# AV on shared query rows and transposes in transpose mode by 64x128 tiles, four head pairs in one burst

## The chip, the cores and the metric

The kernel runs on one core of one Trainium2 chip. The metric is the device time in microseconds of one execution; the kernel before has a median of 320.39 us in three runs (319.56 to 322.47). Each kernel has one profiled execution besides, from which all views of the profile come.

The engines are called as the profile calls them: PE is TensorE's matrix multiplication, PEld its weight load, DVE is VectorE, ACT ScalarE, POOL GpSimd, SP the SyncE queue that issues transfers.

## The reference

An attention of two parts and, on its result, a dense network of two layers. All inputs and the output are fp32; there are 8 images of 576 tokens, 8 heads of 64.

```python
def _attn_ref(q, k, v):
    B, H, S, D = q.shape
    factor = 4
    Sd = S // factor
    scale = 1.0 / np.sqrt(D)
    ...
    q_d = q.reshape(B, H, Sd, factor, D).mean(axis=3)
    k_d = k.reshape(B, H, Sd, factor, D).mean(axis=3)
    v_d = v.reshape(B, H, Sd, factor, D).mean(axis=3)
    out_d = sm_attn(q_d, k_d, v_d)
    out_up = np.repeat(out_d, factor, axis=2)
    pos = np.arange(S)
    mask = np.abs(pos[:, None] - pos[None, :]) < factor
    scores = scale * np.matmul(q, k.transpose(0, 1, 3, 2))
    scores = np.where(mask, scores, -1000000000.0)
    ...
    out_local = np.matmul(attn, v)
    return (out_up + out_local).astype(np.float32)

def _moe_ref(x, w_in, w_out):
    h = x @ w_in
    g = h * (1.0 / (1.0 + np.exp(-1.702 * h)))
    return (g @ w_out).astype(np.float32)
```

The **down** part is full attention among 144 tokens, each the mean of four, and its result is repeated four times. The **local** part lets each token see the tokens up to 3 places off. x, 4608 tokens by 512 features, is their sum; the network goes 512 to 2048 to 512.

## The kernel before

**Dense layers.** The 4608 tokens are done in nine groups of 512 (`for g in range(n_groups)`). In a group `mm1` makes 16 blocks of 128 hidden features; a block is four 128x512 matmuls, one for each of the four `xT` tiles (features on partitions, tokens along the row), and an ACT `silu` takes it out of PSUM. The first two blocks of a group go together, xT by xT: eight matmuls, two on each xT in order of head pair. `mm2` then makes four blocks of 128 tokens, each of 16 matmuls, and ACT evacuates each block (`store`, L766) and SP sends it out. Blocks take turns on two PSUM banks, `PM`. In group 0 the order in mm2 is its own, with two of the blocks in `PA[0]`.

**Attention** of image g+1 is put between the dense matmuls of group g; image 0 has a version of its own ahead of group 0 (`av_local0`, `av_down0`, `transp_sum`, L518 to L606), which the change does not touch. `attention` gives a list of steps; `POS` (groups 1 to 6) and `POS_0` (group 0) say before which dense matmul each is emitted: a number under 16 is a block of mm1, a number n of 16 or more is matmul n - 16 of mm2. All engines run in the order in which the code emits their instructions; nothing is reordered by a scheduler. Semaphore waits are put in by the framework, which follows tiles: an instruction waits for whoever last used the tile that it touches.

Heads are done in four pairs (`hp`), heads 2hp and 2hp+1. The steps for one image are:

- `s_pe(0)`, `s_act(0)`, `s1`: scores of heads 0 to 3 and then 4 to 7 (L361, L375), local ones in five chunks of 2 x 60 query rows, down ones in three blocks of 48 keys; ACT takes the exponent (L415, L421), and DVE masks the local ones (L429).
- `avn`: AV for two pairs and its `normalise`. `av_local` (L440) multiplies chunk by chunk, `av_down` (L454) block by block, all in 64x64 tiles of the PE array, into a PSUM tile `o` of two banks: seven slots of 65 columns in each bank, the 65th being the sum of the weights. In the lower and the upper 64 partitions of a slot stand the two heads of the pair. `normalise` (L476) is a reciprocal and one multiplication on DVE, into `y` (bf16).
- `tr`: `transp` (L491) turns y by multiplication with an identity, 26 matmuls of 64x64 tiles for a pair, into an fp32 PSUM tile `x` of its own; the head goes to the right 64 partitions there. Then `copy_od` (L620) copies the down result, repeated four times, from `x` to `od` (fp32 in SBUF, two ACT copies), and `merge` (L637) adds the local result from `x` and `od` into `xT` (two DVE additions, of 570 and of 6 columns).

In groups 1 to 6 the last steps are `avn(0, 1)`, then AV of pairs 2 and 3 with the transposes of pair 0, then the transposes of pairs 1 to 3 with their additions. In group 0 they are `avn(0, 1)`, `tr(0)`, `tr(1)`, `avn(2, 3)`, `tr(2)`, `tr(3)`, each in a place of its own. Three PSUM tiles of two banks, `PA`, serve scores, `o` and `x` in turn (`ps_tile`); in group 0 `o` and `x` use two fixed ones of them. The second of the two first mm1 blocks uses a PA bank too.

DVE's other work for the next image (`prep_qk`, L267) is emitted at the head of the group; POOL pools q and k (L297, L301) and the values (L313, L316) and issues the loads of q and k. SP loads the values (L210, L233).

Of the kernel before, what the change touches and what calls it, by code (L numbers as in the profile page):

```python
# [19 lines left out]
def kernel(  # L20
# [410 lines left out]
    def av(b, hp, n=None):  # L431
        o = ps_tile(n)
        av_local(b, hp, o)
        av_down(b, hp, o)
        return o

    def banks(t):
        return t if t is PM else [t[:, u, :] for u in range(2)]

    def av_local(b, hp, o, chunks=range(5)):  # L440
        E, vb, o = es[hp], vbs[b % 2], banks(o)
        for i in chunks:
            for par in range(2):
                for j in range(2):
                    pos = j if par == 0 else 1 - j
                    nc.tensor.matmul(  # L446
                        o[par][64 * pos : 64 * pos + 64, 65 * i : 65 * i + 65],
                        lhsT=E[64 * par : 64 * par + 64, j, 60 * i : 60 * i + 64],
                        rhs=vb[64 * par : 64 * par + 64, i, 2 * hp + j, :],
                        start=True, stop=True,  # L450
                        tile_position=(64 * par, 64 * pos),
                    )

    def av_down(b, hp, o):  # L454
        Ed, vd, u, o = eds[hp // 2], vds[b % 2], hp % 2, banks(o)

        blocks = [(kc, x, 0) for kc in range(3) for x in range(2)]
        blocks += [(0, 0, 1), (0, 1, 1), (1, 0, 1), (2, 0, 1)]
        if True:
            for kc, x, c2 in blocks:  # L460
                for j in range(2):
                    pos = j if x == 0 else 1 - j
                    c0 = 65 * (5 + c2)
                    q0 = SD * kc + 48 * (min(x + c2, 1) + x)
                    last = x == c2 == 1
                    if last:
                        q0 = 0
                    nc.tensor.matmul(  # L468
                        o[j][64 * pos : 64 * pos + 64, c0 : c0 + 65],
                        lhsT=Ed[64 * j : 64 * j + 48, u, q0 : q0 + 64],  # L470
                        rhs=vd[64 * j : 64 * j + 48, kc, hp, :],
                        start=(kc == 0), stop=(kc == 2 or last),
                        tile_position=(64 * j, 64 * pos),
                    )

    def normalise(o):  # L476
        y = work.tile([128, 2, 7, D], BF16, name="y", tag="y", bufs=4)
        rc = work.tile([128, 2, 7, 1], FP32, name="rc", tag="rc")
        for xs in (slice(0, 1), slice(1, 2)) if o is PM else (slice(0, 2),):
            n = xs.stop - xs.start  # L480
            ov = (o[xs.start][:, None, :] if o is PM else o)[:, :, 0:455].rearrange(
                "p x (c e) -> p x c e", e=65
            )
            nc.vector.reciprocal(rc[:, xs], ov[:, :, :, 64:65])
            nc.vector.tensor_tensor(  # L485
                out=y[:, xs], in0=ov[:, :, :, 0:D],
                in1=rc[:, xs].to_broadcast([128, n, 7, D]), op=ALU.mult,
            )
        return y

    def transp(y, n=None):  # L491
        x = ps_tile(n)
        for i in range(5):
            for par in range(2):
                for j in range(2):
                    pos = j if par == 0 else 1 - j
                    c0 = 0 if (par == 1 or i == 0) else 3
                    c1 = 60 if (par == 0 or i == 4) else 57
                    nc.tensor.matmul(  # L499
                        x[64 * j : 64 * j + 64, par, 57 * i + c0 : 57 * i + c1],  # L500
                        lhsT=y[64 * pos : 64 * pos + 60, par, i, :],
                        rhs=ident(pos, 60, c0, c1),
                        start=True, stop=True,
                        tile_position=(64 * pos, 64 * j),
                    )
        for c2, xx in ((0, 0), (0, 1), (1, 0)):
            for j in range(2):
                pos = j if xx == 0 else 1 - j
                nc.tensor.matmul(  # L509
                    x[64 * j : 64 * j + 64, xx, 288 + 48 * c2 : 336 + 48 * c2],  # L510
                    lhsT=y[64 * pos : 64 * pos + 48, j, 5 + c2, :],
                    rhs=ident(pos, 48, 0, 48),
                    start=True, stop=True,
                    tile_position=(64 * pos, 64 * j),
                )
        return x
# [103 lines left out]
    def copy_od(x):  # L620
        od = work.tile([128, S], FP32, name="od", tag="od")
        for xx, t0, n in ((0, 0, 96), (1, 96, 48)):
            nc.scalar.copy(  # L623
                out=od[:, 4 * t0 : 4 * (t0 + n)].rearrange("p (t f) -> p t f", f=4),
                in_=x[:, xx, 288 : 288 + n, None].to_broadcast([128, n, 4]),
            )
        return od
# [351 lines left out]
```

## Time and profile before

| | |
|---|---|
| median of three runs | 320.39 us (319.56 to 322.47) |
| the profiled execution's own time | 320.13 us |
| its span, first to last instruction | 318.4 us |
| PE, PEld busy | 301.9 us (95%), 156.5 us (49%) |
| ACT, POOL, DVE busy | 184.9 us (58%), 138.7 us (44%), 130.3 us (41%) |
| mean granted TensorE clock | 0.995 |
| dense matmuls 128x512 (L717, L781) | 576 in each layer (the last block in halves) |
| transposes (L499, L509) | 560 and 168 matmuls |
| additions into xT (L644, L650) | 28 of 752 ns, 28 of 169 ns |

The profile gives for each instruction its start, its duration and what it waited for. The matmuls overlap in the array, so that a dense one lasts 379 ns in the profile while the next starts 216 ns after it; what an instruction costs the row is the distance between starts, not its duration. "Issue" is time in which an engine waited for nothing that the profile shows. The remainder of the execution's time, 1.7 us, lies before the first and after the last instruction.

### The profile page before, as it was taken

Reading aid. Unit: us, or ns where it says so; the run is one execution under the profiler, and the core shown is the slowest. Engines: PE = TensorE matmul, PEld = TensorE weight load, DVE = VectorE, ACT = ScalarE, POOL = GpSimd, SP = SyncE. Lnnn points to the kernel's source line nnn. Section 1 sums busy time; section 2 is a strip of 40 time slices with the busy share of each in tenths; the row PEclk is TensorE's granted clock in tenths of the full one; section 3 lists DMA queues with packets and bytes.
Section 4 is the critical chain, followed back from the end, with each engine's and each line's share of the span. In section 5 each row is a group of like instructions: output and inputs, shape, how many; then the busy total and the mean of one; then the engine's idle time right before and its main releaser. Section 6 shows DMA issues by size and latency. Waiting matters only on the chain.

```text
span 318.4 us, 10941 instructions
## 1 busy us (share of the span) xinstructions
PE 301.9 (95%) x4872; PEld 156.5 (49%) x4923; DVE 130.3 (41%) x219; ACT 184.9 (58%) x320; POOL 138.7 (44%) x170
## 2 busy tenths in 40 slices
PE   7699999999899999999999999999999999999995
PEld 4465454545454555445545454445445544444444
DVE  5855625831575047704780288017811650000000
ACT  5445782567546684659465846584667556415611
POOL 8773790099227940695059604980294000000000
PEclk9979999999999999999999999999999999999999
DMA  7999999999949923995299619961810210020011
GB/s 120 118 200 209 182 126 213 166 229 227 165 128 203 207 64 103 190 209 101 72 197 205 128 48 213 206 136 39 176 41 3 70 68 2 0 99 33 2 65 67
DMA packets 64078, 40.02 MB, mean 126 GB/s; under 512 B 44064, under 2 KB 55456, under 8 KB 64032
## 3 DMA queue, kind: packets, MB, share of 16 engines
q1 hardware_dynamic: 44496, 24.32, 37.3%
q0 software_dynamic: 19392, 14.95, 33.8%
q8 instruction: 38, 0.62, 0.9%
q14 instruction: 8, 0.07, 0.1%
q10 hardware_dynamic: 144, 0.07, 0.1%
HBM read 44.83 MB, written 9.44 MB: 170 GB/s over the span
## 4 chain that ended last, share of the span: by engine, by line
PE 91%; issue 3%; DMA 2%; DVE 1%; POOL 1%; ACT 1%; POOLq 0%
PE pm L781 35%; PE pm L717 35%; PE pa L717 4%; PE pa L365 2%; PE pa L377 2%; DMA qb<-in_q_dram 2%; PE pa L781 2%; PE pa L446 2%; PE pa L499 2%; PE pa L468 2%; PE pm L796 1%; PE pm L334 1%; PE pa L509 0%; PE pa L524 0%; DVE qT L267 0%
## 5 line engine op out<-in xcount | busy, mean ns | idle before, releaser
L717 PE MATMUL pm<-xT,w_in_bf 128*128 128x512 bf16 x495 | 118.2, 379 | 1.2 <-ACT xT L616 0.2
L781 PE MATMUL pm<-w_out_bf,gT 128*128 128x512 bf16 x499 | 114.4, 379 | 4.2 <-issue 4.1
L728 ACT ACTIVATE gT<-pm 128x512 bf16<-128x512 f32 x128 | 76.3, 598 | 43.7 <-PE pm L717 43.7
L717 PEld LDWEIGHTS <-w_in_bf 128*128 128x128 bf16 x576 | 55.7, 98 | 66.5 <-issue 0.5
L781 PEld LDWEIGHTS <-gT 128*128 128x128 bf16 x560 | 52.1, 98 | 60.1 <-issue 0.8
L429 DVE TENSOR_TENSOR es<-es,mask 128x600 bf16<-128x600 bf16 x28 | 17.6, 643 | 94.6 <-ACT es L415 93.8
L297 POOL TENSOR_TENSOR pq<-kT 128x576 f32<-128x576 bf16 x13 | 15.1, 1165 | 70.5 <-DVE kT L267 70.5
L766 ACT ACTIVATE osb<-pm 128x512 f32<-128x512 f32 (+2 forms) x35 | 20.5, 586 | 38.2 <-PE pm L781 30.3
L623 ACT COPY od<-pa 128x384 f32<-128x384 f32 (+1 forms) x56 | 19.0, 407 | 27.2 <-PE pa L509 20.7
L485 DVE TENSOR_TENSOR y<-pa,rc 128x896 bf16<-128x896 f32 x28 | 30.6, 1092 | 1.0
L415 ACT ACTIVATE es<-pa 128x600 bf16<-128x600 f32 x32 | 19.7, 668 | 9.5 <-PE pa L365 9.4
L644 DVE TENSOR_TENSOR xT<-pa,od 128x570 bf16<-128x570 f32 x28 | 21.0, 752 | 8.8 <-ACT od L623 8.8
L313 POOL TENSOR_TENSOR v<-v 112x512 f32<-112x512 f32 x18 | 23.0, 1279 | 0.0
L768 DVE TENSOR_SCALAR osb<-pm 128x128 f32<-128x128 f32 x1 | 0.3, 291 | 55.0 <-ACT osb L766 55.0
L267 DVE STREAM_TRANSPOSE kT<-kb 128x576 f32<-128x576 f32 x16 | 20.0, 1250 | 4.3 <-DMA kb<-in_k_dram 4.2
L267 DVE STREAM_TRANSPOSE qT<-qb 128x576 f32<-128x576 f32 x16 | 19.9, 1242 | 0.6 <-POOL kdT L301 0.2
L717 PE MATMUL pa<-xT,w_in_bf 128*128 128x512 bf16 x64 | 20.0, 379 | 0.0
L307 POOL CAST vb<-vf 128x2560 bf16<-128x2560 f32 x6 | 13.9, 2319 | 13.7 <-DMA vf<-in_v_dram 11.3
L365 PEld LDWEIGHTS <-kT 32*64 32x64 bf16 x1280 | 14.2, 104 | 7.7 <-issue 4.9
L365 PE MATMUL pa<-qT,kT 32*64 32x60 bf16 x1280 | 16.4, 198 | 1.3 <-DVE qT L267 1.3
L221 POOL DMA_DIRECT2D vb<-in_v_dram x20 | 13.7, 698 | 9.1 <-DMA w_in_bf<-in_moe_w_in_dram 4.0
L297 POOL TENSOR_TENSOR pq<-qT 128x576 f32<-128x576 bf16 x14 | 16.0, 1145 | 0.1
(90 smaller groups left out, 274.2 us busy)
## 6 DMA issues: line engine op xcount, KB each, us to landing
out_dram<-osb SPq DMA_DIRECT2D x35, 256.0 KB, 2.1
vf<-in_v_dram SPq DMA_DIRECT2D x60, 128.0 KB, 6.8
v<-in_v_dram SPq DMA_DIRECT2D x36, 192.0 KB, 5.5
kb<-in_k_dram POOLq DMA_DIRECT2D x16, 288.0 KB, 7.2
qb<-in_q_dram POOLq DMA_DIRECT2D x16, 288.0 KB, 8.6
w_in_bf<-in_moe_w_in_dram POOLq DMA_DIRECT2D x4, 512.0 KB, 7.2
w_out_bf<-in_moe_w_out_dram POOLq DMA_DIRECT2D x4, 512.0 KB, 12.9
vb<-in_v_dram POOLq DMA_DIRECT2D x20, 64.0 KB, 6.4
```

What stands on the lines that cost most here:

```text
L267: nc.vector.transpose(out=t32.rearrange("p (i c) -> p c i", c=18), in_=store[b, qd].bitcast(FP32).rearrange("p (c d) -> p c d", c=18),)
L297: nc.gpsimd.tensor_tensor(out=t1, in0=sv[:, :, 0:2, :], in1=sv[:, :, 2:4, :], op=ALU.add)
L313: eng.tensor_tensor(out=t1[0:112], in0=x[:, :, 0:2, :], in1=x[:, :, 2:4, :], op=ALU.add)
L365: nc.tensor.matmul(sp[r // 2][64 * par : 64 * par + 64, r % 2, 60 * i : 60 * i + 60], lhsT=kT[b, qd][rows, k0 : k0 + 64, a], rhs=qT[b, qd] ...
L415: nc.scalar.activation(out=es[2 * qd + u][:, :, 0:300], in_=sp[u][:, :, 0:300], func=AF.Exp, scale=inv_sqrt_d,)
L485: nc.vector.tensor_tensor(out=y[:, xs], in0=ov[:, :, :, 0:D], in1=rc[:, xs].to_broadcast([128, n, 7, D]), op=ALU.mult,)
L623: nc.scalar.copy(out=od[:, 4 * t0 : 4 * (t0 + n)].rearrange("p (t f) -> p t f", f=4), in_=x[:, xx, 288 : 288 + n, None].to_broadcast([128, ...
L644: eng.tensor_tensor(out=sub(xT[hp], t0 + 3, (57, 2), (114, 5), (1, 57)), in0=sub(x, 3, (509, 2), (57, 5), (1, 57)), in1=sub(od, 3, (57, 2) ...
L717: nc.tensor.matmul(acc, lhsT=w_in_bf[:, dmc, ffc * 128 : (ffc + 1) * 128], rhs=xT[dmc][:, g * TG : g * TG + TG], start=(dmc == 0), stop=(d ...
L728: nc.scalar.activation(out=gT[:, ffc, :], in_=acc, func=AF.Silu, scale=GELU_SCALE)
L766: eng.activation(out=osb, in_=ap, func=AF.Copy, scale=1.0 / GELU_SCALE)
L781: nc.tensor.matmul(ops[t], lhsT=gT[:, ffc, t * 128 : (t + 1) * 128], rhs=w_out_bf[:, ffc, :], start=(ffc == 0), stop=(ffc == n_ffc - 1),)
```

## The change

- **AV.** In `av` the two heads of a pair now share the partitions of a slot: the lower 64 partitions hold the even chunks and the upper ones the odd chunks, of both heads side by side. Chunk i of head j goes to slot `i // 2 * 2 + j` (one further on for the second half). The down blocks are laid out in the same manner, 64 query rows each, with the odd ends in slots of their own. The number and shape of the matmuls stay, their order is new.
- **normalise** writes the same columns, and an ACT copy of 64 columns on the upper partitions (`y[64:128, 5]` from `y[64:128, 12]`) is added behind it.
- **transp** takes 60 or 64 query rows of both heads in one instruction, 128 columns on a 64x128 tile, in transpose mode, into a PSUM tile seen as bf16. There are 13 for a pair, and two pairs share one PSUM tile (`x_pair`).
- **copy_od** and **merge**: od is bf16; the copies are of 64 and 80 columns repeated four times (96 and 48 before); the addition becomes three, of 456, 117 and 3 columns.
- **Steps.** All images have the same six steps: the transposes of all four pairs are one step at the end, and the additions follow. `POS` moves scores of heads 4 to 7 from 35 to 33, AV from 45 to 44 and the last step from 69 to 67; `POS_0` drops three steps, and has AV at 46 and 57 (46 and 56 before) and the transposes at 68.

```diff
     def av(b, hp, n=None):
         o = ps_tile(n)
-        av_local(b, hp, o)
-        av_down(b, hp, o)
+        E, Ed, vb, vd, u = es[hp], eds[hp // 2], vbs[b % 2], vds[b % 2], hp % 2
+
+        def local(i, par, j):
+            pos, c0 = i % 2, 65 * (i // 2 * 2 + j + par)
+            nc.tensor.matmul(
+                o[64 * pos : 64 * pos + 64, par, c0 : c0 + 65],
+                lhsT=E[64 * par : 64 * par + 64, j, 60 * i : 60 * i + 64],
+                rhs=vb[64 * par : 64 * par + 64, i, 2 * hp + j, :],
+                start=True, stop=True,
+                tile_position=(64 * par, 64 * pos),
+            )
+
+        def down(kc, j, pos, slot, q0, last=2):
+            nc.tensor.matmul(
+                o[64 * pos : 64 * pos + 64, j, 65 * slot : 65 * slot + 65],
+                lhsT=Ed[64 * j : 64 * j + 48, u, SD * kc + q0 : SD * kc + q0 + 64],
+                rhs=vd[64 * j : 64 * j + 48, kc, hp, :],
+                start=(kc == 0), stop=(kc == last),
+                tile_position=(64 * j, 64 * pos),
+            )
+
+        for i in (0, 2):
+            for j in range(2):
+                for par, e in ((0, 0), (1, 1), (1, 0), (0, 1)):
+                    local(i + e, par, j)
+        left = [(local, (4, par, j)) for j in range(2) for par in range(2)]
+        left += [(down, (kc, j, 0, 6 - 6 * j, 0)) for kc in range(3) for j in range(2)]
+        right = [(down, (0, j, 1, 5 + j, 64, 0)) for j in (1, 0)]
+        right += [(down, (kc, j, 1, 6 - 6 * j, 64)) for kc in range(3) for j in (1, 0)]
+        right += [(down, (kc, j, 1, 4 + j, 128)) for kc in range(3) for j in (1, 0)]
...
     def normalise(o):
...
+        nc.scalar.copy(out=y[64:128, 5, :], in_=y[64:128, 12, :])
+        return y
+
+    def x_pair(n=None):
+        t = ps_tile(n).rearrange("p x n -> p (x n)").bitcast(BF16)
+        t = t.rearrange("p (x n) -> p x n", x=2)
+        return [t[:, :, 512 * u : 512 * u + 512] for u in range(2)]
+
+    def transp(y, x):
+        def put(pos, c0, n, src):
+            nc.tensor.matmul(
+                x[:, pos, c0 : c0 + n], lhsT=src, rhs=ident(pos, src.shape[0], 0, n),
+                is_transpose=True, start=True, stop=True, tile_position=(64 * pos, 0),
+            )
+
+        for m in range(3):
             for par in range(2):
...
+                for pos in range(2 if m < 2 else 1):
+                    c0 = 8 * par + 2 * m
+                    put(pos, 120 * m + 60 * par, 60, y[64 * pos : 64 * pos + 60, c0 : c0 + 2, :])
+                if m == 2:
+                    c0 = 6 - 2 * par
+                    put(1, 240 + 64 * par, 64, y[64:128, c0 : c0 + 2, :])
+        put(0, 360, 64, y[0:64, 6:8, :])
...
     def copy_od(x):
-        od = work.tile([128, S], FP32, name="od", tag="od")
-        for xx, t0, n in ((0, 0, 96), (1, 96, 48)):
+        od = work.tile([128, S], BF16, name="od", tag="od")
+        for xx, c0, t0, n in ((0, 360, 0, 64), (1, 240, 64, 80)):
...
+    def merge(b, hp, x, od):
         t0 = b * S
...
+        row = x.ap[1][0]
+        for at, col, dims, from_x in (
+            (3, 3, ((228, 2), (114, 2), (1, 114)), ((120, 2), (row, 2), (1, 114))),
+            (459, 243, ((1, 117),), ((1, 117),)),
+            (0, 0, ((1, 3),), ((1, 3),)),
+        ):
+            nc.vector.tensor_tensor(
+                out=sub(xT[hp], t0 + at, *dims), in0=sub(x, col, *from_x),
+                in1=sub(od, at, *dims), op=ALU.add,
+            )
...
+        def tr():
+            for u in range(2):
+                st["x", 2 * u], st["x", 2 * u + 1] = x_pair(slots and slots[u])
+            for hp in range(HP):
+                transp(st["y", hp], st["x", hp])
+            for hp in range(HP):
+                merge(b, hp, st["x", hp], copy_od(st["x", hp]))
+
+        return [lambda: s_pe(0), lambda: s_act(0), s1, avn(0, 1), avn(2, 3), tr]
...
-    POS = [13, 16, 35, 45, 56, 69]
-    POS_0 = [16, 18, 30, 46, 52, 56, 65, 71, 75]
+    POS = [13, 16, 33, 44, 56, 67]
+    POS_0 = [16, 18, 30, 46, 57, 68]
     VDP_0 = 41
```

## The prediction

> **What bounds the kernel now.** I read the page first, then the chain that ended last in order of time, then timelines of single stretches, and last the rows of single lines.
>
> ```profile
> PE 301.9 (95%) x4872; PEld 156.5 (49%) x4923; DVE 130.3 (41%) x219; ACT 184.9 (58%) x320; POOL 138.7 (44%) x170
> ...
> PE 91%; issue 3%; DMA 2%; DVE 1%; POOL 1%; ACT 1%; POOLq 0%
> ```
>
> TensorE is the bound: busy for 95%, and 91% of the chain. The granted clock is 0.995. So an edit is worth what it takes out of, or puts into, the row of TensorE's instructions; DVE (41%) and ACT (58%) count only where TensorE waits for them. The chain in order of time, in one image (the columns: start, us, what):
>
> ```profile
> 148.25 2.10 PE pm L781 x9
> ...
> 151.34 2.32 PE pm L781 x10
> ...
> 154.85 2.75 PE pm L781 x12
> ...
> 158.54 2.32 PE pm L781 x10
> ```
>
> A 128x512 matmul of the dense layers takes one step of 0.2158 us (31 of them 6.69 us in the same view). Between them stand bursts of attention, and a burst costs the gap between the end of the last step and the next dense matmul: AV of two pairs 150.19 to 151.34, 1.15; AV of two pairs with one pair's transposes 153.50 to 154.85, 1.35; the transposes of three pairs 157.44 to 158.54, 1.10. Transposing an image thus costs 0.20 + 1.10 = 1.30 us. In group 0, which does image 1, each pair is transposed in a burst of its own:
>
> ```profile
> 50.56 1.03 PE L781 MATMUL pm<-w_out_bf,gT 128*128 128x512 bf16 x4
> ...
> 52.41 1.04 PE L781 MATMUL pm<-w_out_bf,gT 128*128 128x512 bf16 x4
> ...
> 53.94 1.67 PE L781 MATMUL pa<-w_out_bf,gT 128*128 128x512 bf16 x7 [0.16 <-issue]
> ...
> 56.81 1.24 PE L781 MATMUL pm<-w_out_bf,gT 128*128 128x512 bf16 x5 [0.16 <-issue]
> ...
> 58.75 0.81 PE L781 MATMUL pa<-w_out_bf,gT 128*128 128x512 bf16 x3
> ...
> 60.05 1.03 PE L781 MATMUL pa<-w_out_bf,gT 128*128 128x512 bf16 x4 [0.16 <-issue]
> ```
>
> By the same reckoning 0.99 (with a wait inside), 0.67, 0.63 (the next dense matmul is at 58.52) and 0.65: 2.94 us.
>
> **AV.** 40 matmuls for a pair before and 40 after, all of 64x65 or 48x65 on four 64x64 tiles, the busiest tile with 11 in both; only order and place change. Cost nothing. If the new order put neighbours on one tile, the last four would lose some 0.03 us each; I keep 0.2 us an image in the range.
>
> **The transposes.** 26 for a pair on four 64x64 tiles become 13 on two tiles of 64x128, seven on the first and six on the second. The 1.10 us of three pairs are 0.10 before the first, 0.65 in which 78 start (some 20 on each tile, so 0.033 us a step), and 0.35 from the last start to the next dense matmul. The trace has one row of 64x128 tiles:
>
> ```profile
> 21.86 0.27 PE L547 MATMUL pa<-vd,ed 48*128 48x65 bf16 x6
> ```
>
> Each takes 0.19, so six start within 0.08 us, three on each tile: 0.037 a step. With 60 columns for 65 I take 0.035. Four pairs are 28 steps on the fuller tile, 0.98 us, and the burst 0.10 + 0.98 + 0.35 = 1.43. Half the instructions, but half the tiles: the stream is no shorter. Transpose mode is not in this trace. Bounds: as dense as the 64x64 ones (52 x 0.0083 = 0.43, burst 0.88), or one after the other as the full-array transposes of L600 (eight in 0.29, 0.036 each; 1.87, burst 2.32).
> Group 0: 1.43 - 2.94 = **-1.51**. The six others: +0.13 each, **+0.8**.
>
> **What follows the burst.** The next layer's first eight matmuls go through the four xT in order, two on each, and nothing else is queued on TensorE behind them that could go first. For each pair ACT copies the down part to od, then DVE adds. The timeline of the burst above:
>
> ```profile
> 158.04 1.31 ACT L623 COPY od<-pa 128x384 f32<-128x384 f32 x4 [0.88 <-PE pa L509]
> 159.84 0.70 ACT L623 COPY od<-pa 128x384 f32<-128x384 f32 x2 [0.49 <-DVE xT L650]
> ...
> 158.77 0.75 DVE L644 TENSOR_TENSOR xT<-pa,od 128x570 bf16<-128x570 f32 x1 [1.02 <-ACT od L623]
> 159.56 0.17 DVE L650 TENSOR_TENSOR xT<-pa,od 128x6 bf16<-128x6 f32 x1
> ```
>
> Copies to the first add 0.73 (two copies, 576 elements before and after); adds 0.96 to their end; a copy that waited for an add starts 0.11 after it. Today DVE ends at 161.53, and the seventh matmul wants the last xT at 160.86 + 1.30 = 162.16: 0.6 us to spare.
>
> After the change two pairs share a PSUM tile, and in the built order pair 1's copy waits for pair 0's adds, pair 3's for pair 2's. The chain becomes copy, add, copy, add (with pair 2's copies beside pair 1's adds), copy, add. What an add costs is the open term. Three rows of tensor_tensor, beside L644 above:
>
> ```profile
> L429 DVE TENSOR_TENSOR es<-es,mask x28: 458/472/1884, 41.9 to 248.4; 128x600 bf16<-128x600 bf16 x28
> L485 DVE TENSOR_TENSOR y<-pa,rc x28: 1091/1092/1093, 50.2 to 254.8; 128x896 bf16<-128x896 f32 x28
> L129 DVE TENSOR_TENSOR dm<-dm 128x60 f32<-128x60 f32 x1 | 0.2, 220 | 1.1 <-POOL dm L108 1.1
> ```
>
> L485 (fp32 from PSUM), L129 (fp32 from SBUF) and L644 lie on one line, 0.157 + 1.04 ns an element, so PSUM by itself costs nothing here. L429, all bf16, is at 0.157 + 0.52 ns. The new adds are bf16 throughout, PSUM included, so I take the second line, as the type is what sets these rows apart: 456, 117 and 3 elements are 0.39, 0.22 and 0.16. Without a wait between them DVE starts one 0.08 before the last one's end (y at 155.79 for 1.09, the next at 156.80), so 0.61 for a pair. On the first line: 0.63, 0.28, 0.16, together 0.91. That is the other end.
> The Trainium skill, "VectorE: DVE Perf Modes", section "The perf-mode tier table", speaks for that other end: it puts tensor_tensor with any PSUM operand at 1x. "Vector Engine (DVE) Microarchitecture Reference", section 5.1, asks for 2-byte operands and unit steps alone. No row here shows bf16 from PSUM; by the first rule the sum is rival one's.
>
> From the first transpose as zero: pairs 0 and 1 transposed 14 x 0.035 + 0.19 = 0.68; copies 0.78; adds 1.51 to 2.12; copies 2.23, adds 2.96 to 3.57; pair 2's adds follow at once, to 4.15; copies 4.26, adds 4.99 to 5.60; TensorE some 0.05 later: 5.65. TensorE: burst over at 0.98 + 0.35 = 1.33, 13 dense matmuls to 4.14, and the seventh of the next layer at 5.44. It stands **0.21** us; in group 0, with 12 matmuls, **0.43**. Together +1.7. The first three xT come in time.
>
> **The scores of heads 4 to 7** move from dense matmul 19 of mm2 to 17.
>
> ```profile
> 146.07 0.90 ACT L421 ACTIVATE ed<-pa 128x864 bf16<-128x864 f32 x1
> ...
> 147.04 0.33 PE L365 MATMUL pa<-qT,kT 32*64 32x60 bf16 x32
> 147.28 0.27 PE L377 MATMUL pa<-qdT,kdT 32*64 32x144 bf16 x4
> ```
>
> The down scores (L377) go into the tile that this exp reads until 146.97. Two steps earlier they would be due at 146.85 and wait to some 147.03: **+0.2** us in six groups, +1.2; the rest of the burst is queued behind them. In group 0 the step stays. Bounds 0 and 0.3.
>
> **Nothing on the path.** The new ACT copy in normalise (64 elements; by the od rows of 0.33 for 192 and 0.48 for 384, some 0.23) waits for DVE; behind it ACT holds at most the evacuation of one output bank, which TensorE wants again 16 steps (3.5 us) later. Without that cover TensorE would stand some 1.5 us. Pair 3's y is ready 2.5 us after the second AV burst, its transposes come 11 steps (2.4) and 0.6 later. DVE's preparation for the next image starts 0.4 us or so later against TensorE; POOL ends at 145.7 what AV wants at 150.3. load_v4 goes out two steps earlier on SP, for work some 14 us later. AV of pairs 0 and 1 keeps 11 steps behind the scores, where it had 10.
>
> **Sum.** -1.5 + 0.8 + 1.7 + 1.2 = +2.2 on the profiled execution's 320.13 (span 318.4, 1.7 around it): 322.3. The median of the three is 320.39, 0.26 above it; some of TensorE's idle time inside bursts (below) may go with fewer instructions. I say **322.0**.
>
> **Rivals.**
> One: the adds run at one element a step, 0.91 a pair. Then they end at 6.83; TensorE stands 1.4 us in six groups and 1.6 in group 0, so -1.5 + 0.8 + 10.0 + 1.2 = +10.5: **330.6**. The place is the same eight matmuls; each 0.1 us more on the adds of a pair, beyond some 0.56, adds 0.4 there. For it: every PSUM row in the trace is at this rate. Against: all of those are fp32.
> Two: transpose mode does not run two tiles side by side. The burst is 2.32, +1.02 for each of six and -0.6 in group 0, but the adds then end in time (6.1 against 6.3): with the scores' wait +6.7, **326.8**. Against: L547 overlaps.
> Three, faster: waits of 0.2 us are within my reading of edges of 0.1; both may be nothing, which leaves -0.7, and AV bursts that cost 2.21 instead of 1.15 at 83 us and 1.74 at 88 us (idle put down to issue, 0.88 us in one place) may lose theirs, worth up to 2.1 in all: **317.3 to 319.4**. For it: a tenth fewer PE instructions between dense matmuls. Against: the idle stands in AV, which keeps its count.
> That the transposes are halved but give nothing is in the forecast itself.
>
> **Numbers.** Forecast 0.56 (its own range 320 to 324); rival one 0.20; two 0.10; three 0.14. About 1% (3.2 us) is what a measurement of this kernel can tell from no change. Faster: a quarter of three, 0.04. Slower: one, two and a sixth of the forecast, 0.38. Same: 0.58. The range 318.3 to 330.0 leaves out the fast half of three, more than half of one and the forecast's edges.
>
> **What would show it.** Rows of the new add with 456 elements: 0.39 or 0.63. The transposes' step on one tile, and a burst of 1.43. A gap before the seventh matmul of mm1, and one before the first L377 of the second scores. Wrong if the gap before mm1 is over 1 us or absent, or if the output banks' evacuation holds TensorE.

## The result and the profile after

The changed kernel took 323.61 us (median of six runs, 321.96 to 325.62) against 319.85 for the kernel before beside it: a ratio of 1.0106, interval 1.0071 to 1.014. In a second series, with other kernels, it took 322.34 (twelve runs) against 320.79: 1.0059 [1.0035, 1.0083]. So it is slower, by 0.6 to 1.1%. The profiled execution took 322.25 us, its span is 320.5, the granted clock 0.995 as before.

The page after, with the same two lines as before the change:

```profile
PE 301.8 (94%) x4509; PEld 154.9 (48%) x4559; DVE 124.1 (39%) x247; ACT 189.9 (59%) x348; POOL 138.8 (43%) x170
...
PE 63%; ACT 11%; DVE 11%; issue 7%; DMA 4%; SPq 1%; POOL 0%; DVEq 0%; ACTq 0%; POOLq 0%
```

TensorE is busy for as long as before (301.9, now 301.8). What changed is the second line: before, 91% of the chain that ended last was TensorE; now ACT and DVE hold 11% each. Somewhere TensorE has begun to wait for them. The view of what TensorE waits for (us in total, times, the longest) names where:

```profile
PE pm L744 <- issue: 4.3, 27, 0.2
PE pm L680 <- DVE xT L630: 2.4, 6, 0.4
...
PE pa L377 <- ACT ed L421: 1.0, 6, 0.2
```

The last two have no counterpart before: there no wait for DVE's xT stands in the list, and none of the down scores for the exp. (L680 is the first layer, before L717; L744 the second, before L781; L630 the adds; L488 the transposes.)

One image, TensorE's timeline. The columns are start, duration of the group, what, and in brackets the idle time before it:

```profile
122.14 1.03 PE L744 MATMUL pm<-w_out_bf,gT 128*128 128x512 bf16 x4
123.09 0.96 PE L488 MATMUL pa<-id,y 60*128 60x60 bf16 x52
124.21 2.75 PE L744 MATMUL pm<-w_out_bf,gT 128*128 128x512 bf16 x12 [0.16 <-issue]
...
127.88 0.38 PE L680 MATMUL pa<-xT,w_in_bf 128*128 128x512 bf16 x1
128.68 0.38 PE L680 MATMUL pm<-xT,w_in_bf 128*128 128x512 bf16 x1 [0.42 <-DVE xT L630]
```

From 127.88 to 128.68 are 0.80 us where a dense step is 0.22: TensorE stands 0.58 us before the seventh matmul of the first layer, the first that reads the last pair's xT. (The 0.42 in brackets is shorter because a matmul's record goes on after the next could start; gaps below are always start to start, less one step.) ACT and DVE beside it:

```profile
123.11 0.24 ACT L478 COPY y<-y 64x64 bf16<-64x64 bf16 x1 [1.04 <-DVE y L474]
123.37 0.60 ACT L729 ACTIVATE osb<-pm 128x512 f32<-128x512 f32 x1
123.87 0.70 ACT L608 COPY od<-pa 128x256 bf16<-128x256 bf16 x2
125.28 1.31 ACT L608 COPY od<-pa 128x256 bf16<-128x256 bf16 x4 [0.71 <-DVE xT L630]
127.30 0.70 ACT L608 COPY od<-pa 128x256 bf16<-128x256 bf16 x2 [0.72 <-DVE xT L630]
```

```profile
124.60 0.59 DVE L630 TENSOR_TENSOR xT<-pa,od 128x456 bf16<-128x456 bf16 x3 [1.52 <-ACT od L608]
126.01 1.20 DVE L630 TENSOR_TENSOR xT<-pa,od 128x456 bf16<-128x456 bf16 x6 [0.82 <-ACT od L608]
128.03 0.59 DVE L630 TENSOR_TENSOR xT<-pa,od 128x456 bf16<-128x456 bf16 x3 [0.82 <-ACT od L608]
```

Read the brackets crosswise: ACT waits 0.71 for DVE's xT, DVE 0.82 for ACT's od, and again. Pairs 0 and 1 share a PSUM tile, as do 2 and 3, and the built program lets the copy of the second pair begin only when the adds of the first are done. That is the alternation copy, add, copy, add (pair 2's copies beside), copy, add, and its last add ends at 128.63.

Group 0, where four bursts of transposes became one:

```profile
54.07 1.03 PE L744 MATMUL pm<-w_out_bf,gT 128*128 128x512 bf16 x4
55.03 0.96 PE L488 MATMUL pa<-id,y 60*128 60x60 bf16 x52
56.15 0.59 PE L744 MATMUL pm<-w_out_bf,gT 128*128 128x512 bf16 x2 [0.16 <-issue]
56.96 0.38 PE L744 MATMUL pm<-w_out_bf,gT 128*128 128x512 bf16 x1 [0.21 <-issue]
...
59.98 0.38 PE L680 MATMUL pa<-xT,w_in_bf 128*128 128x512 bf16 x1
60.49 0.38 PE L680 MATMUL pm<-xT,w_in_bf 128*128 128x512 bf16 x1
```

The burst costs 1.22, and the wait for the last xT here is 0.30. But TensorE itself comes 0.38 late to it: from 56.36, the second dense matmul shown behind the burst, to 56.96 are 0.60 us for one step, and the trace puts that idle down to issue. In a second profile of the same kernel this idle is absent, and TensorE waits so much the longer:

```profile
60.20 0.38 PE L680 MATMUL pa<-xT,w_in_bf 128*128 128x512 bf16 x1
61.09 0.38 PE L680 MATMUL pm<-xT,w_in_bf 128*128 128x512 bf16 x1 [0.51 <-DVE xT L630]
```

From 60.20 to 61.09 are 0.89 us, a wait of 0.67. So the price of the wait in group 0 is 0.67; in the first profile 0.38 of it is hidden behind other idle time. (On the order in group 0: in `POS_0` the AV of pairs 2 and 3 stood at 65 before the change; the 56 there was the transposes of pair 1.)

**Where the time went.** I take the loop: from the first dense matmul behind the first scores of group 0 to the end of the span. It leaves out the start, which varies by 2 us and more between profiles (the loop begins at 40.19 before, at 39.28 and 39.88 in two profiles after, at 42.00 in one further kernel). Before, it is 278.16 us, after 281.20, and 280.41 in the second profile of the same changed kernel. In it some bursts are longer than others of their kind by idle that the trace puts down to issue, of another size in each profile: 2.21 us before, 1.66 and 0.51 after. Of the 1.66 the 0.38 in group 0 cost nothing, as the wait for xT would have taken that time anyway. Without the rest (2.21, 1.28 and 0.51) the loop is 275.95 before, and 279.92 and 279.90 after: **+4.0 us**. The places, added up gap by gap:

| place | before | after | difference |
|---|---|---|---|
| transposes of group 0 | 2.48 | 1.00 | -1.48 |
| six images: AV and transposes | 1.14 + 1.36 + 1.10 | 1.16 + 1.16 + 1.21 | -0.4 |
| AV of group 0 | 2 x 1.14 | 2 x 1.16 | +0.0 |
| second scores, six images | 1.31 | 1.57 | +1.6 |
| wait for the last xT, group 0 | 0 | 0.67 (0.30 and 0.38 hidden) | +0.7 |
| wait for the last xT, six images | 0 | 0.52, and 0.58 five times | +3.4 |
| two small gaps in group 0, behind that wait | 0 | 0.05 + 0.12 | +0.2 |

The sum is +4.0, so nothing is left over. Two things have to be known for the first row. The first of its bursts before (0.98) holds a wait that the trace puts down to issue:

```profile
52.27 0.21 PE L509 MATMUL pa<-id,y 48*64 48x48 bf16 x3 [0.37 <-issue]
```

The third burst, which has all its records too, costs 0.63. If the 0.35 between them is chance idle as well, the row is -1.1 and the change +4.3; there is one profile of the kernel before, so this stays open. The other thing is that the trace misses the record of one dense matmul behind most bursts: after the last burst of an image the order of the work has 13 matmuls of the second layer (scheduled at 67 of 80), the timeline shows 12. A cost read from gap to gap then holds one step (0.216) of work. The traces of the two last kernels below have those records, and there AV of two pairs costs 0.93 where the others show 1.16, and the burst of 52 transposes 0.99 where they show 1.22. Of the four bursts before in group 0 (0.98, 0.65, 0.63, 0.65) the second and fourth lack such a record (8 dense matmuls shown where the order has 9, and 4 where it has 5), so they cost 2.91 - 0.43 = 2.48; the one after costs 1.22 - 0.22 = 1.00.

### The profile page after: what moved, and what is told of

It is laid out like the page before. It is cut to its first block, busy times and chain, and to the rows that moved or that the text cites. A ratio compares the mean times of both kernels' runs of the same rounds, so it can differ in the third digit from the quotient of the medians.

```text
span 320.5 us, 10251 instructions
## 1 busy us (share of the span) xinstructions
PE 301.8 (94%) x4509; PEld 154.9 (48%) x4559; DVE 124.1 (39%) x247; ACT 189.9 (59%) x348; POOL 138.8 (43%) x170
## 4 chain that ended last, share of the span: by engine, by line
PE 63%; ACT 11%; DVE 11%; issue 7%; DMA 4%; SPq 1%; POOL 0%; DVEq 0%; ACTq 0%; POOLq 0%
PE pm L680 29%; PE pm L744 19%; DVE y L474 4%; DVE xT L630 4%; ACT od L608 4%; DMA vf<-in_v_dram 3%; PE pa L680 3%; ACT es L415 3%; ACT L650 2%; PE pa L377 2%; PE pa L437 2%; PE pa L365 2%; PE pa L744 2%; DMA qb<-in_q_dram 2%; ACT ed L421 1%
## 5 line engine op out<-in xcount | busy, mean ns | idle before, releaser
L680 PE MATMUL pm<-xT,w_in_bf 128*128 128x512 bf16 x495 | 118.3, 379 | 3.8 <-DVE xT L630 2.4
L744 PE MATMUL pm<-w_out_bf,gT 128*128 128x512 bf16 x499 | 114.4, 379 | 4.5 <-issue 4.3
L680 PEld LDWEIGHTS <-w_in_bf 128*128 128x128 bf16 x576 | 55.5, 97 | 70.5 <-issue 5.5
L744 PEld LDWEIGHTS <-gT 128*128 128x128 bf16 x560 | 52.2, 98 | 61.4 <-issue 1.2
L429 DVE TENSOR_TENSOR es<-es,mask 128x600 bf16<-128x600 bf16 x28 | 19.5, 720 | 89.5 <-ACT es L415 89.0
L478 ACT COPY y<-y 64x64 bf16<-64x64 bf16 x28 | 6.7, 240 | 34.6 <-DVE y L474 34.6
L630 DVE TENSOR_TENSOR xT<-pa,od 128x456 bf16<-128x456 bf16 (+2 forms) x84 | 16.6, 255 | 22.1 <-ACT od L608 22.0
L608 ACT COPY od<-pa 128x256 bf16<-128x256 bf16 (+1 forms) x56 | 18.9, 409 | 9.9 <-DVE xT L630 9.9
L680 PE MATMUL pa<-xT,w_in_bf 128*128 128x512 bf16 x64 | 20.0, 379 | 0.0
```

The lines of the kernel that those rows point to most:

```text
L429: nc.vector.tensor_tensor(out=ev, in0=ev, in1=mask, op=ALU.mult)
L608: nc.scalar.copy(out=od[:, 4 * t0 : 4 * (t0 + n)].rearrange("p (t f) -> p t f", f=4), in_=x[:, xx, c0 : c0 + n, None].to_broadcast([128, n ...
L630: nc.vector.tensor_tensor(out=sub(xT[hp], t0 + at, *dims), in0=sub(x, col, *from_x), in1=sub(od, at, *dims), op=ALU.add,)
L680: nc.tensor.matmul(acc, lhsT=w_in_bf[:, dmc, ffc * 128 : (ffc + 1) * 128], rhs=xT[dmc][:, g * TG : g * TG + TG], start=(dmc == 0), stop=(d ...
L744: nc.tensor.matmul(ops[t], lhsT=gT[:, ffc, t * 128 : (t + 1) * 128], rhs=w_out_bf[:, ffc, :], start=(ffc == 0), stop=(ffc == n_ffc - 1),)
```

## The experiments

All are edits of the changed kernel, except where another is named. Each ratio is against the kernel before on the same chip.

### The changed kernel once more

> The changed kernel itself, beside the other three on one chip. Both theories (the wait for the last xT and the scores' wait; or a cost in the bursts themselves): its loop shows a gap of 0.5 to 0.6 us before the seventh matmul of mm1 in six groups and second scores of 1.57; time 321.5 to 325 us. If the idle that the trace puts down to issue in the AV bursts sits at other bursts and has another size than in the first profile of the same kernel, it is noise of an execution and no part of the change.

Measured: 322.34 us, ratio 1.0059 [1.0035, 1.0083]. The gaps (0.52, then 0.57 or 0.58 five times) and the second scores (1.57) are those of the first profile; in group 0 the wait is 0.67, as shown above. The longer AV bursts are not: 1.64, 1.56 and 1.43 there, 1.21 and 1.50 here, with 1.16 for the rest. That idle is no part of the change.

### Pairs that share a tile kept apart

```diff
-                st["x", 2 * u], st["x", 2 * u + 1] = x_pair(slots and slots[u])
-            for hp in range(HP):
+                st["x", u], st["x", 2 + u] = x_pair(slots and slots[u])
+            for hp in (0, 2, 1, 3):
                 transp(st["y", hp], st["x", hp])
```

Pairs 0 and 2 share a tile, and 1 and 3; copies and adds keep the order 0, 1, 2, 3. Nothing else moves.

> The changed kernel with one edit: pairs 0 and 2 share one PSUM tile and pairs 1 and 3 the other (transposed in the order 0, 2, 1, 3), where pairs 0 and 1, and 2 and 3, shared one. Theory: the gap of 0.58 us before the next layer's seventh matmul comes from copies and adds taking turns, because copy and add of neighbouring pairs touch one tile; apart, pair 1's copy runs beside pair 0's adds, the adds follow each other at some 0.55 to 0.6 us, the last ends some 1.4 us earlier and the gap is gone in all seven groups (-3.5 to -4 us): about the time of the kernel before (ratio 0.998 to 1.003). Rival: the copies and adds of four pairs are too much work behind one burst whatever their order; then the gap stays above 0.3 us and the time falls by less than 1.5 us (ratio above 1.006).

Measured: 319.25 us, ratio 0.9947 [0.9913, 0.998]. No gap for xT is left in any image, and the list of TensorE's waits no longer has DVE's xT in it. The same stretch on ACT and DVE:

```profile
125.35 2.72 ACT L608 COPY od<-pa 128x256 bf16<-128x256 bf16 x8
```

```profile
126.08 1.20 DVE L630 TENSOR_TENSOR xT<-pa,od 128x456 bf16<-128x456 bf16 x6 [1.52 <-ACT od L608]
127.49 1.20 DVE L630 TENSOR_TENSOR xT<-pa,od 128x456 bf16<-128x456 bf16 x6 [0.21 <-ACT od L608]
```

All eight copies run in one stretch of 2.72 us and DVE waits 0.21 instead of 0.82 between pairs: from the first copy to the last add 3.3 us where the changed kernel takes 4.8. The loop without issue idle is 275.7, against 279.9: the sharing of tiles by neighbours in the order was the whole of the wait, and the two small gaps in group 0 go with it. (A shared tile is also a shared pair of PSUM banks here; the runs don't tell the two apart.) The loop is only 0.3 under that of the kernel before, the measured time 1.3; the traces don't show where the rest comes from.

### The scores back to their step

```diff
-    POS = [13, 16, 33, 44, 56, 67]
+    POS = [13, 16, 35, 44, 56, 67]
```

> The changed kernel with the scores of heads 4 to 7 put back from 33 to 35 in POS. Theory: their burst costs 1.57 us in place of 1.31 because its down scores wait for the exponent that still reads their PSUM tile; two steps later it costs 1.31 again, -1.6 us in all, ratio to the kernel before 1.004 to 1.007, and the gap before the seventh matmul of the next layer stays at 0.58. Rival: the burst waits for POOL's pooled q and k, which start later against TensorE than before; then it waits as long in absolute time, and the burst costs 1.4 or more still, no gain above 0.6 us.

Measured: 322.56 us, ratio 1.0055 [1.0025, 1.0085]. The second scores cost 1.31 again (1.40 in one image), where the changed kernel has 1.57. There, the down scores wait for the exp that reads their tile:

```profile
112.11 0.33 PE L365 MATMUL pa<-qT,kT 32*64 32x60 bf16 x32
112.61 0.26 PE L377 MATMUL pa<-qdT,kdT 32*64 32x144 bf16 x4 [0.17 <-ACT ed L421]
```

and here they do not:

```profile
112.03 0.33 PE L365 MATMUL pa<-qT,kT 32*64 32x60 bf16 x32
112.27 0.27 PE L377 MATMUL pa<-qdT,kdT 32*64 32x144 bf16 x4
```

The gap for xT stays (0.47 to 0.58). The loop without issue idle is 278.2: 1.7 less than the changed kernel, for six times 0.26.

### Both

> The changed kernel with both edits, pairs apart and scores at 35. If both theories hold the gains add up: -5 to -5.5 us from the changed kernel, ratio to the kernel before 0.993 to 0.998. If the later scores push the work behind them into the end of the group, less than the sum.

The edit is the two above together. Measured: 319.32 us, ratio 0.9962 [0.9924, 1.0001]. Neither wait is left, and the loop without issue idle is 274.1: the two gains add up (279.9 less 4.2 and 1.7 is 274.0). That loop is 1.85 us, 0.6%, under that of the kernel before, which is what the merged bursts save once nothing waits: 1.48 in group 0 (1.1 if the wait of 0.37 before was chance) and 0.4 in the other six images. The interval of the measured ratio just reaches 1, so the time alone doesn't show a gain.

### The adds with an fp32 operand

```diff
-        od = work.tile([128, S], BF16, name="od", tag="od")
+        od = work.tile([128, S], FP32, name="od", tag="od")
```

The down part that DVE adds is kept in fp32; the other operand, from PSUM, and the result stay bf16.

> The changed kernel with od in fp32 in place of bf16, so that the adds have operands of two types. Theory: the adds then go at one element a step, 0.63 us for 456 columns in place of 0.40, 0.28 for 117 in place of 0.21; four chained adds are 1.2 us later, the gap before the next layer's matmuls grows from 0.58 to about 1.8 us in seven groups, +8 us, ratio 1.03 to 1.04: what rival one of the prediction would have cost. Rival: the rate of the adds is set by the bf16 PSUM operand and not by all types together; then they stay at 0.40 and the time is that of the changed kernel.

Measured: 330.05 us, ratio 1.0285 [1.0228, 1.0342]. The adds in the changed kernel and in this one (count, total and mean in ns; the types shown are those of the output and of the first operand):

```profile
L630 DVE TENSOR_TENSOR xT<-pa,od 128x456 bf16<-128x456 bf16 x28 | 11.3, 404 | 22.1 <-ACT od L608 22.0
L630 DVE TENSOR_TENSOR xT<-pa,od 128x117 bf16<-128x117 bf16 x28 | 5.9, 210 | 0.0
L630 DVE TENSOR_TENSOR xT<-pa,od 128x3 bf16<-128x3 bf16 x28 | 4.2, 151 | 0.0
```

```profile
L630 DVE TENSOR_TENSOR xT<-pa,od 128x456 bf16<-128x456 bf16 x28 | 17.7, 632 | 22.0 <-ACT od L608 22.0
L630 DVE TENSOR_TENSOR xT<-pa,od 128x117 bf16<-128x117 bf16 x28 | 7.5, 269 | 0.0
```

From 117 to 456 elements the first goes from 210 to 404 ns, 0.57 ns an element; the second from 269 to 632, 1.07. One fp32 operand nearly halves the rate, and each pair's adds grow by 0.29; the copies to od keep their time (376 ns for 128x256 in both). TensorE then waits 0.36 and 1.28 in an image where it waited 0.58. So the adds stand on the path in this arrangement, and at the fp32 rate they cost about what rival one said; in the changed kernel they run at the bf16 rate.

### Four pairs in one burst undone

```diff
+        def av_tr():
+            for hp in (2, 3):
+                st["o", hp] = av(b, hp)
+            st["x", 0], st["x", 1] = x_pair()
+            for hp in (0, 1):
+                transp(st["y", hp], st["x", hp])
+            for hp in (2, 3):
+                st["y", hp] = normalise(st["o", hp])
+            for hp in (0, 1):
+                merge(b, hp, st["x", hp], copy_od(st["x", hp]))
...
-        return [lambda: s_pe(0), lambda: s_act(0), s1, avn(0, 1), avn(2, 3), tr]
+        first = [lambda: s_pe(0), lambda: s_act(0), s1, avn(0, 1)]
+        return first + ([avn(2, 3), tr] if b == 1 else [av_tr, tr23])
```

tr23 does pairs 2 and 3 in the last burst. The shared tiles and the scores stay as the change has them.

> Four pairs in one burst undone alone: in six images pairs 0 and 1 are transposed in the burst of AV of pairs 2 and 3 (as pair 0 was before), pairs 2 and 3 in the last burst; the tiles stay shared as in the changed kernel (0 with 1, 2 with 3), the scores stay where the change put them. Theory one (the wait before mm1's seventh matmul comes from two copy-and-add turns of shared tiles that all start with the last burst): the last xT is then ready about 3.7 us after the burst's first transpose, the seventh matmul comes at about 4.7, so the gap of 0.58 goes in six groups; 3.5 us less than the changed kernel, about the first experiment's time (319 to 320.5); the AV burst grows by 0.4 to 0.8, the last shrinks by 0.4. Rival (the cost is the turn from one tile shape or mode to another): AV burst and transposes together cost over 1 us more in an image than apart, and the time stays at 322 to 324.

Measured: 323.68 us, ratio 1.0103 [1.006, 1.0146]. The theory failed: the gap before the seventh matmul is still 0.48, and the first scores of an image are 0.22 later as well. ACT's timeline says why:

```profile
122.84 0.24 ACT L478 COPY y<-y 64x64 bf16<-64x64 bf16 x1 [1.46 <-DVE y L474]
124.11 0.24 ACT L478 COPY y<-y 64x64 bf16<-64x64 bf16 x1 [1.04 <-DVE y L474]
124.38 0.70 ACT L608 COPY od<-pa 128x256 bf16<-128x256 bf16 x2
125.79 0.70 ACT L608 COPY od<-pa 128x256 bf16<-128x256 bf16 x2 [0.71 <-DVE xT L630]
126.38 0.62 ACT L748 ACTIVATE osb<-pm 128x512 f32<-128x512 f32 x1
126.87 0.72 ACT L608 COPY od<-pa 128x256 bf16<-128x256 bf16 x2
128.30 0.70 ACT L608 COPY od<-pa 128x256 bf16<-128x256 bf16 x2 [0.71 <-DVE xT L630]
```

The transposes of pairs 0 and 1 are over at 122.2, but their copies stand in ACT's queue behind the change's small y copies of pairs 2 and 3, which wait for DVE. All four turns of copy and add begin at 124.38, 2.2 us after those transposes and only 0.2 before the last burst (124.60), so little is won over one burst. The rival, a cost of going from one tile shape to the other, is too small to matter: with the missing record allowed for, AV with transposes and the last burst are 1.44 + 0.59, against 0.94 + 1.00 apart, +0.09 an image.

### The y copy on DVE

```diff
-        nc.scalar.copy(out=y[64:128, 5, :], in_=y[64:128, 12, :])
+        nc.vector.tensor_copy(out=y[64:128, 5, :], in_=y[64:128, 12, :])
```

> The changed kernel with the 64-element copy inside normalise on DVE and not on ACT. Theory: in the changed kernel this copy waits on ACT for DVE's multiplication and holds an output bank's evacuation (0.60) behind it, which ends 0.1 us after the first od copy could start; with the copy on DVE the od copies start some 0.13 earlier, and the gap before mm1's seventh matmul falls from 0.58 to about 0.45 in six groups: 0.8 us of 322, seen in the trace rather than in the time. Rival (the first copy waits for the transposes themselves): the gap stays 0.58, or grows by the copy's time on DVE, some 0.1.

Measured: 322.38 us, ratio 1.0056 [1.002, 1.0092]; the gap falls from 0.58 to 0.45 or 0.46 in five of the six images; the first has none, because its burst of transposes was itself 0.46 longer. In group 0 it is 0.57 for 0.67. In the changed kernel the y copy of pair 3 ends at 123.35, an output bank's evacuation of 0.60 follows, and only then the od copies. Now the evacuation no longer stands between:

```profile
122.81 0.60 ACT L729 ACTIVATE osb<-pm 128x512 f32<-128x512 f32 x1 [3.97 <-PE pm L744]
124.00 0.70 ACT L608 COPY od<-pa 128x256 bf16<-128x256 bf16 x2 [0.59 <-PE pa L488]
```

and the copies wait for the transposes alone. The theory holds: 0.12 of the 0.58 was the y copy, with the evacuation behind it.

### Tiles apart, scores back, y copy on DVE

> Tiles shared by pairs 0 and 2 and by 1 and 3, the scores of heads 4 to 7 back at step 19, and the y copy on DVE. Theory: without a wait for xT left, an earlier copy gains nothing: the loop from group 0's scores to the end is 274 us without the idle put down to issue, as in the third experiment, against 279.7 in the changed kernel and 275.6 before; time 317.5 to 320, about 1.5% under the changed kernel and 0.5% under the kernel before. Rival (chain to xT still on the path somewhere): a gain of 0.8 us or more over the third experiment.

Measured: 319.65 us, ratio 0.9974 [0.9942, 1.0005]; 0.8% under the changed kernel on the same chip, where 1.5% was expected. The loop without issue idle is 274.1, exactly that of both edits without this one: with no wait for xT left, the earlier copy gains nothing. The issue idle in this profile is 3.7 us, against 0.5 in the changed kernel's beside it; that covers part of the gain, and the expected time had not allowed for it.

### Two bursts with the y copy on DVE

> The two bursts of the fifth experiment, with the y copy on DVE and not on ACT. Theory: there the od copies of pairs 0 and 1 stood on ACT behind the y copies of pairs 2 and 3, which wait for DVE until 124.1, so all four turns of copy and add began 1.5 us after they could, and the last xT came as late as with one burst. Without that the first od copies start some 0.6 us after the transposes of pairs 0 and 1, beside DVE's normalise, the last add ends some 0.7 us before TensorE wants it, and the gap of 0.48 before the seventh matmul goes; DVE reaches the next image's preparation a microsecond earlier, so the first scores cost 1.08 again and not 1.30. Loop 277.5 to 278.5 without large issue idle, 3.5 to 4 us under the fifth experiment; time 319 to 320.5. Rival (the turn from one tile shape to the other costs, or the adds themselves are too slow): gap and time as in the fifth experiment, 322.5 to 324.

Measured: 322.55 us, ratio 1.0037 [1.0001, 1.0072]. In the trace the mechanism holds in the main, in the time it does not show. The wait for xT is gone in four of the six images (0.03 is left). In the first it is 0.24, where one y copy took 0.82 instead of 0.18 on DVE, and in the second it is 0.30:

```profile
122.89 0.70 ACT L608 COPY od<-pa 128x256 bf16<-128x256 bf16 x2 [2.51 <-PE pa L488]
126.27 0.70 ACT L608 COPY od<-pa 128x256 bf16<-128x256 bf16 x2 [2.68 <-DVE xT L630]
```

```profile
122.36 0.25 DVE L473 RECIPROCAL rc<-pa 128x14 f32<-128x14 f32 x1
...
123.97 0.25 DVE L473 RECIPROCAL rc<-pa 128x14 f32<-128x14 f32 x1
124.25 1.09 DVE L474 TENSOR_TENSOR y<-pa,rc 128x896 bf16<-128x896 f32 x1
125.38 0.18 DVE L478 COPY y<-y 64x64 bf16<-64x64 bf16 x1
125.59 0.59 DVE L630 TENSOR_TENSOR xT<-pa,od 128x456 bf16<-128x456 bf16 x3
```

This is the image with the 0.30. Pair 0's copies now start when its transposes are done (122.89), but its adds wait on DVE for two turns of normalise, which the y copy has made longer: 1.61 us from one reciprocal to the next where it was 1.29. (In the images without a wait the turns are as long, but DVE pauses 0.4 or more between the second and the third.) The loop is 280.64, and 2.9 of it is idle that other bursts of the same kind don't have (2.72 against 0.93 in the third AV burst alone); without it 277.7, where 277.5 to 278.5 was expected. Whether the larger issue idle comes with this order or is chance, one profile doesn't tell, and the time is that of the changed kernel.

### All of it

> All of it: two bursts, y copy on DVE, scores of heads 4 to 7 back at step 19, group 0 with its four pairs in one burst on tiles shared by 0 and 2 and by 1 and 3. Theory: no wait left, and AV with transposes 2.25 an image against 2.37 in two bursts of their own: loop 0.7 us under that of the third and seventh experiments less issue idle, 273.4; time 317.5 to 319.5, under both kernels. Rival (noise of start and issue idle covers it): the same time as the third and seventh experiments, 319.3 to 319.7, and an interval that reaches 1.

Measured: 321.16 us, ratio 0.9988 [0.9952, 1.0024]. The expectation failed. Two bursts cost 0.09 more an image than two of their own, not 0.12 less: I had compared a burst with a missing record to one without. The longer turns on DVE make transposes wait for y (0.7 us in two places), 0.25 and 0.30 for an xT are left in two images, and the issue idle is again large. It is no better than the two plain edits.

### Which version is best

The version that beats the kernel before most clearly is the plainest, the pairs kept apart (0.9947 [0.9913, 0.998]); with the scores back as well the traces show 1.6 us less still, but the measured times don't (319.25 and 319.32 us), and none of these versions is over 0.6% faster than the kernel before.

## Why the prediction came out as it did

The forecast was 322.0, no change or slightly slower; it became 323.61, and 322.34 in the second series. The likeliest case happened: the merged burst gave its saving in group 0, and two new waits took it back and more. The nearness of the number is partly luck. The terms added up to +2.2, and the traces show +4.0 in the loop; the profiled execution still came out at 322.25, beside the sum's 322.3, because its loop began 0.9 earlier than before the change and held 0.9 less of the issue idle that counts. The step that was mis-sized is the wait for the last xT. Step by step:

**AV.** Said: nothing. It is 1.14 before and 1.16 after, +0.02 a burst.

**The transposes.** The term of the step was too high: 0.035 us a step on the fuller tile, taken from a row of another 64x128 operation. The 52 transposes start within 0.77 us (123.09 for 0.96, the last taking 0.19), 28 steps, so 0.0275. The burst is 1.22 and not 1.43. For the six other images +0.8 was said and -0.4 measured: 0.21 of it in each, 1.3 together, is this step. For group 0, -1.51 was said and -1.48 measured, but by two errors that cancel: -0.2 for the step, +0.2 because four bursts before hid two dense matmuls and the one after hides one.

**The wait for the last xT.** The mechanism and the place were right, and so was the length of the chain: 5.65 us from the first transpose to TensorE was said, 5.58 measured (123.09 to 128.68), the adds 0.39, 0.22 and 0.16 against 0.404, 0.210 and 0.151. Two errors cancel in its first link, though: the transposes of pairs 0 and 1 are over 0.1 sooner than said, and the first copy is held 0.12 by an evacuation that the sum left out (below), so it starts at the 0.78 that was said. The term that was mis-sized is when TensorE wants it, 5.44: it comes at 5.00, 0.21 earlier because the burst is shorter and 0.22 earlier because the 13 matmuls behind the burst were counted in full although the one without a record had already been counted into the burst's cost. So 0.58 for 0.21, and +4.1 for +1.7. In the six images the shorter burst gained nothing: what it saved, the wait took. In group 0 the same sum gave 0.43, and the wait is 0.67; the first profile's 0.30 comes from TensorE's own 0.38 of delay.

**The scores.** 0.2 was said and 0.26 measured, six times, and the step back takes it away. Right.

**Nothing on the path.** This failed in one place. The y copy was put at 0.23 behind the cover of an evacuation that TensorE wants late (measured 0.24). What stands behind the evacuation was left out: the od copies, the first link of the chain to xT. It costs 0.12 an image, and in the arrangement with two bursts it holds back all four turns.

**The rivals.** One, adds at one element a step: the rows exclude it, and the fp32 experiment gives about its price, 330.05 for 330.6; from the changed kernel (322.34) that is +7.7 where the prediction had 8.6 between the two. The Trainium skill, "VectorE: DVE Perf Modes", section "The perf-mode tier table", has 1x for tensor_tensor with any PSUM operand; the 404 ns for 456 elements against 632 with one fp32 operand disagree. Another section of that page of the Trainium skill, "Why PSUM operands drop a tier", allows a 2x form from PSUM and 1x for fp32; the 404 ns agree with it. The Trainium skill, "Vector Engine (DVE) Microarchitecture Reference", section 5.1, asks for two-byte types in all operands for that form, and both rows agree with it.
Two, transposes that don't run side by side: excluded, 52 of them start within 0.77 us where one after the other was put at 1.87, and the first ones start in pairs 2 to 4 ns apart. Three, no waits: the waits are there, and larger; the issue idle in the AV bursts did not go (1.64 in one of them where 1.16 is usual).

## What to carry over

Two outputs that share a PSUM tile also shared its release in this program: if two engines read the tile in turns, put into one tile those that are not neighbours in the order of the readers. A burst that is merged for TensorE's sake moves the first moment at which its readers can start; add up the chain behind the last of its parts against the first instruction that needs it, and name everything that stands in each reader's queue, small copies included. And before costs are read from gaps in a trace, count the instructions in them against the program: here a missing record made 0.22 us of work look like idle time, and it was counted twice.

## What was not expected of the hardware

- A tensor_tensor of bf16 throughout, with one operand in PSUM, takes 0.57 ns an element (210 ns for 117, 404 for 456), and 1.07 when the other operand is fp32.
- Transposes of 60x128 in transpose mode start every 0.0275 us on one 64x128 tile, two tiles side by side, quicker than the matmuls of 48x65 on such tiles had suggested (0.037).
- A copy of 64 elements that takes DVE 0.18 us makes a turn of dependent instructions there 0.32 longer (1.29 to 1.61).
- The idle put down to issue comes at the same places of the program in most profiles, the third AV burst and the one near 218 us and, in most, the dense stretch behind group 0's transposes, with sizes from nothing to 1.8 us. What it is stays open; it puts from 0.5 to some 4 us into the loop, so two profiles can differ by as much as the change itself is worth.
